# Pooling sums by accumulating DMAs, block-diagonal q and low weight parts on VectorE in an attention and feed-forward kernel on one core

## The chip, the core and the metric

One core of a Trainium2 chip runs the whole program. A core has TensorE (PE; its weight loads are listed as PEld), VectorE (DVE), ScalarE (ACT), GpSimd (POOL) and SyncE (SP), which here only issues DMAs. Each has a queue of its own and works through it in order; semaphores let one wait for another. 16 DMA engines move data between the memory outside (HBM) and the on-chip memory SBUF. TensorE writes its results to a second on-chip memory, PSUM.

The metric is the device time of one execution in microseconds, as the median of several runs. The profile shows one execution; its span runs from the first to the last instruction of the program, and the time of a run contains a few microseconds more around it.

## The reference

Eight batches, eight heads, 576 positions, 64 values per head. Two attentions are added: one over positions pooled by four (q, k and v averaged over four neighbours, 144 positions, full softmax), repeated four times along the positions, and a local one in which a position sees its neighbours at a distance below four. The sum goes through a feed-forward layer of 512 -> 2048 -> 512 with a leaky step.

```python
q_d = q.reshape(B, H, Sd, factor, D).mean(axis=3)      # factor = 4, Sd = 144
k_d = k.reshape(B, H, Sd, factor, D).mean(axis=3)
v_d = v.reshape(B, H, Sd, factor, D).mean(axis=3)
out_d = sm_attn(q_d, k_d, v_d)
out_up = np.repeat(out_d, factor, axis=2)
mask = np.abs(pos[:, None] - pos[None, :]) < factor
scores = np.where(mask, scale * np.matmul(q, k.transpose(0, 1, 3, 2)), -1e9)
out_local = np.matmul(softmax(scores), v)
x = (out_up + out_local).transpose(0, 2, 1, 3).reshape(B * S, H * D)   # 4608 x 512
h = x @ w_in
return np.maximum(0.01 * h, h) @ w_out
```

## The kernel before

**Stages.** The columns of x (4608 of them, one per position) are cut into chunks. Chunks 0 and 1 (256 and 320 columns) are batch 1; chunks 2 to 12 (256, 320, then 384 each) are cut from batches 2 to 8. In the code batches count from 0, so batch 2 is `b == 1`, and `BANDED = 1` says that batch 1 alone takes the banded way (local attention by matmuls, `banded`). For the others the local attention is done on POOL and DVE: `scores` multiplies q with seven shifted k on POOL (L560) and sums on DVE (L566), a softmax of small steps follows, `values` multiplies and sums again (L621, L627), and `landing` turns the result on PE (L658), adds the pooled part (L665) and splits it into a high part xh on ACT (L671) and a low part xl on DVE (L673). One unit of this work is a segment of at most `MAXSEG` blocks (a block is 64 columns) and one half `u` of the heads, with one load each of q, k and v. Tiles q, k and v have one buffer each, so a load of k waits for the last product that reads the one before.

**Feed-forward.** x and the weights are split into high and low parts of a fast matmul type, and each product is made of three matmuls: `up_proj` (L698), the leaky step on ACT (L708, L709) and DVE (L711), `down_proj` (L738). Chunks 0 and 1 pass over the first and the second half of the 2048 hidden values apart, as the weights arrive; each later chunk takes one pass. x has two buffers, so chunk n+2 is filled while chunk n+1 is used.

**Weights.** `convert` loads a quarter of w_in (k = 0) or of w_out (k = 1) at a time into a staging tile (it borrows the buffers of k, v, prod, up and, early, of chunk 1's x), rebuilds the values on ACT (L266) and DVE (L268), writes the high part on ACT (w_in, L279) or DVE (w_out, L276) and the low part `lo` on POOL (L281), 32 times in all. The last of these ends at 113 us, and the first product L560 follows it.

**Pooled attention.** `pooled(b, c)` handles two heads (c of NC = 4). `fetch` loads q and k side by side, [128, 2, 576], and v as [72, 2, 2, 64, 4] with the four neighbours innermost. For batches 2 to 8 DVE sums the four neighbours (L338 into qk_d, L380 into v_d). PE makes scores in six products of 64 rows and 64 columns each, one per head and third of q (L351). The softmax works over PSUM on DVE and ACT, three transposes of weights per half go through PE (L390) and ACT (L392), and four products mix v_d (L402); ACT copies the result out (L407) to outd. `widen` repeats it four times (L645).

**What sets the order.** The program is written out by a planner (`Order`) that runs at build time: each piece of work is a generator that yields its engine and an estimated duration; the planner takes the piece that can start first (then by its rank given to `spawn`) and so fixes the order of every engine's queue. Estimates: `COST` per engine, `pe(...)` in microseconds, `load` with 300 kB per microsecond. On the chip the queues are in order, so where something takes longer than planned, all behind it on that engine waits. SP's queue holds all loads and stores.

```python
t = yield from op("DVE", 1152, tq, s_qd.t)
nc.vector.tensor_reduce(out=qk_d, in_=qkr, axis=AX.X, op=ALU.add)              # L338
nc.tensor.matmul(sc[rows, qi * SD:(qi + 1) * SD], qk_d[rows, qi * QB:qi * QB + 64],
                 qk_d[rows, SD:2 * SD], start=True, stop=True)                  # L351, six times
nc.vector.tensor_reduce(out=v_d, in_=vs, axis=AX.X, op=ALU.add)                # L380
```

Of the kernel before, what the change touches and what calls it, by code (L numbers as in the profile page):

```python
# [19 lines left out]
FAC = 4  # L20
# [6 lines left out]
SCALE = 1.0 / D ** 0.5  # L27
MAXSEG = 4
SIZES = (4, 5, 6, 6, 6, 6, 6, 6, 6, 6, 6)
QB = 48  # L30
# [45 lines left out]
HOP = 0.2  # L76
SAFE = 0.4
SCARCE, HURRY = ("pt",), 1000

# [100 lines left out]
@with_exitstack  # L180
def attn_moe(ctx: ExitStack, tc, qkt, vd, qb, kb, vb, vwb, band, identb, w_in, w_out, ident, edge, out):
    nc = tc.nc
# [4 lines left out]

    bufs = dict(head=HEADS, qk=1, vs=1, qk_d=2, v_d=1, su_vd=2, su_half=1, st_d=2, pd=2, ptd=1, outd=2, q=1, k=1, v=1, s=3, st_l=3, prod=2, up=1,
                xloc=2, lst=3, gh=3, gl=3, o=2, hp=2, pt=2, xh0=1, xl0=1, xh1=1, xl1=1, acc0=1, acc1=1, acc2=1, acc3=1,
# [24 lines left out]
    def load(out, in_, size, *after):  # L214
        t = yield ("op", "SP", 0.3, max((0.0,) + after), size)
        nc.sync.dma_start(out=out, in_=in_)
        return t

# [31 lines left out]
    for h in heads:  # L250
        nc.vector.memset(h, 0)

    def convert(f, k):
# [27 lines left out]
        nc.gpsimd.tensor_tensor(out=lo, in0=tf, in1=hi.bitcast(F32), op=ALU.subtract)  # L281
        s.free(t)
# [24 lines left out]

    def fetch(b, c, pool):
        if pool is None:
            sq, sv = (yield from slot(*(("qk", "up") if b < BANDED else ("qk",)))), (yield from slot("vs"))  # L310
            qk, vs = sb(sq, [128, 2, S], F32), sb(sv, [72, 2, 2, D, FAC], F32)
        else:
            sq, sv = None, (yield from slot("su_vs"))
            qk = pool.tile([128, 2, S], F32, name=f"qk{c}")
            vs = sb(sv, [72, 2, 2, D, FAC], F32, pool)
        tq = yield from load(qk, qkt[b, c], 590e3, sq.t if sq else 0.0)
        od.signal(("asked", b, c))
        kept[b, c] = qk
        od.signal(("qk", b, c), tq)
        tv = yield from load(vs, vd[b, c], 295e3, sv.t if sv else 0.0)  # L320
        return sq, sv, qk, vs, tq, tv

    def pooled(b, c, rank, pool=None):
        sq, sv, qk, vs, tq, tv = yield from fetch(b, c, pool)
        s_qd = yield from slot("qk_d")
        qk_d = sb(s_qd, [128, 2 * SD], F32)
        qkr = qk.rearrange("p a (s r) -> p (a s) r", r=FAC)
        if b < BANDED and (b, c) != (0, 0):
            s = yield from slot("su_half")
            half = sb(s, [128, 2 * SD, 2], F32, pool)  # L330
            t = yield from op("POOL", 576, tq, s.t, s_qd.t)
            nc.gpsimd.tensor_tensor(out=half, in0=qkr[:, :, :2], in1=qkr[:, :, 2:], op=ALU.add)
            t = yield from op("POOL", 288, t)
            nc.gpsimd.tensor_tensor(out=qk_d, in0=half[:, :, 0], in1=half[:, :, 1], op=ALU.add)
            s.free(t)
        else:
            t = yield from op("DVE", 1152, tq, s_qd.t)
            nc.vector.tensor_reduce(out=qk_d, in_=qkr, axis=AX.X, op=ALU.add)  # L338
        if sq:
            if b < BANDED:  # L340
                od.spawn(rank, keeper(b, c, sq, t))
            else:
                sq.free(t)
# [3 lines left out]
        t = yield from pe(0.9, t, s_b.t)  # L347
        for qi in range(3):
            for p in range(2):
                rows = slice(64 * p, 64 * p + 64)  # L350
                nc.tensor.matmul(sc[rows, qi * SD:(qi + 1) * SD], qk_d[rows, qi * QB:qi * QB + 64],  # L351
                                 qk_d[rows, SD:2 * SD], start=True, stop=True)
        s_qd.free(t)
        scv = sc[:, :3 * SD].rearrange("p (a s) -> p a s", a=3)
        st, pd = sb(s_st, [128, 2, 3], F32), sb(s_pd, [128, 3, SD], F32)
# [20 lines left out]
        s_st.free(t)  # L376
        s_vd = yield from slot("su_vd" if pool else "v_d")
        v_d = sb(s_vd, [72, 2, 2, D], F32, pool)
        td = yield from op("DVE", 1050, tv, s_vd.t)
        nc.vector.tensor_reduce(out=v_d, in_=vs, axis=AX.X, op=ALU.add)  # L380
        if sv:
            sv.free(td)
# [12 lines left out]
        s_pd.free(tt)  # L395
        to = yield from wait(("outd", b))
        s_b = yield from slot("pt")
        av = bank(s_b)
        t = yield from pe(0.68, te, td, s_b.t)
        for p in range(2):  # L400
            for kc in range(2):
                nc.tensor.matmul(av[64 * p:64 * p + 64, :SD], v_d[:, p, kc], ptd[:, kc, p],  # L402
                                 start=kc == 0, stop=kc == 1)
        s_pt.free(t)
        s_vd.free(t)
        t = yield from op("ACT", 144, t, to)
        nc.scalar.copy(out=outd[b][:, c], in_=av[:, :SD])  # L407
        s_b.free(t)
        od.signal(("pooled", b, c), t)
        if b == 0:  # L410
# [4 lines left out]
    def windows(c, hf, pool):  # L415
        b0, b1 = BLKS[hf]
        s_vw = yield from slot("su_vs" if hf else "su_vw")
        vws[c, hf] = s_vw, sb(s_vw, [WIN, 5, 2, D], F32, pool)
        t = yield from load(vws[c, hf][1][:, :b1 - b0], vwb[0, c, :, b0:b1], 35840 * (b1 - b0), s_vw.t)
        od.signal(("vw", c, hf), t)  # L420
# [370 lines left out]
    with tc.manual_schedule():  # L791
        od.spawn(0, fixed())
        for b in range(B):
            od.spawn(0, outd_tile(b))
# [86 lines left out]
```

## Time and profile before

| | |
|---|---|
| time of three runs | 970.41, 975.27, 976.92 us, median 975.27 |
| span of the profiled execution (its own whole time is not on the page) | 965.5 us |
| PE, DVE, ACT, POOL busy | 936.8, 594.7, 415.6, 611.5 us |
| first projection matmul | 48.5 us |
| last low part of a weight, first product L560 | 113.2, 113.3 us |
| first up projection of chunks 2, 3, 4, 5, 12 | 185.7, 242.0, 306.1, 378.7, 885.1 us |
| last landing of chunk 12 (L673) | 832.8 us |
| last POOL instruction ends | before 808 us |

The page has the span in 40 slices of 24 us; each digit is the busy share of an engine in tenths, PEclk the clock granted to TensorE, DMA the busy share of the DMA engines.

```profile
PE   6699999899999999999999999999999999999997
DVE  5897778767876786687667883872753752411111
ACT  3777655434634454345524552532422423422211
POOL 3655766777989788897889785884685783200000
PEclk9689999999999999999999999999999999999999
DMA  9857656434542543446233542351233221000000
```

How to read it: the first two slices are the start, in which batch 1's attention is done and the first weights arrive; from there on PE is nearly always busy. POOL is at 7 to 9 tenths from slice 7 to the middle and done in slice 34. A row of an engine's list or timeline has the source line, the engine, the operation, the output tile and the inputs, and the shapes (partitions x elements); a busy matmul is shown longer than the distance to the next one, since matmuls overlap, so the distance between starts is what one costs.

### The profile page before, as it was taken

How to read it: one execution, taken by the hardware profiler on the slowest of the kernel's cores; microseconds unless marked ns; L12 is line 12 of the kernel's file. 1: busy time of each engine (PE TensorE's matmuls, PEld its weight loads, DVE VectorE, ACT ScalarE, POOL GpSimd, SP SyncE). 2: the span in 40 equal slices, each digit the busy share in tenths (PEclk: the TensorE clock that was granted, in tenths of full speed). 3: DMA queues.
4: the chain of work that ended last, by engine and by line, in shares of the span. 5: the costliest groups of instructions: out<-in, count | busy, mean ns of one | idle time of the engine just before them, and what ended most of it. 6: DMA issues, size and time to landing. Idle time of an engine off the chain costs nothing.

```text
span 965.5 us, 16163 instructions
## 1 busy us (share of the span) xinstructions
PE 936.8 (97%) x6282; PEld 897.8 (93%) x6282; DVE 594.7 (62%) x895; ACT 415.6 (43%) x1139; POOL 611.5 (63%) x356
## 2 busy tenths in 40 slices
PE   6699999899999999999999999999999999999997
PEld 4499999799999999999999899999999999999997
DVE  5897778767876786687667883872753752411111
ACT  3777655434634454345524552532422423422211
POOL 3655766777989788897889785884685783200000
PEclk9689999999999999999999999999999999999999
DMA  9857656434542543446233542351233221000000
GB/s 261 249 189 238 211 175 196 145 121 136 191 128 87 187 141 105 128 152 188 91 115 115 189 150 96 98 154 60 75 90 99 91 62 46 34 1 1 33 1 33
DMA packets 63180, 117.31 MB, mean 122 GB/s; under 512 B 4944, under 2 KB 32848, under 8 KB 63104
## 3 DMA queue, kind: packets, MB, share of 16 engines
q1 hardware_dynamic: 63104, 116.29, 38.6%
q8 instruction: 49, 0.80, 0.3%
q14 instruction: 27, 0.22, 0.1%
HBM read 105.65 MB, written 10.62 MB: 120 GB/s over the span
## 4 chain that ended last, share of the span: by engine, by line
PE 79%; DMA 8%; POOL 7%; DVE 3%; issue 2%; SPq 1%; ACT 0%; POOLq 0%; DVEq 0%; ACTq 0%
PE hp L698 36%; PE acc L738 35%; POOL prod L560 4%; DMA k<-in_kb_dram 3%; POOL prod L621 2%; PE pt L351 2%; DMA qk<-in_qkt_dram 2%; PE pt L390 2%; PE pt L402 1%; DMA v<-in_w_out_dram 1%; PE pt L658 1%; DMA out_dram<-o 1%; DMA su_vw<-in_vwb_dram 1%; DVE s L566 1%; DMA v<-in_vb_dram 1%
## 5 line engine op out<-in xcount | busy, mean ns | idle before, releaser
L560 POOL TENSOR_TENSOR prod<-q,k 128x1344 f32<-128x1344 f32 (+1 forms) x88 | 260.2, 2958 | 93.3 <-DMA k<-in_kb_dram 61.4
L698 PE MATMUL hp<-xh,wih 128*128 128x384 f32 (+2 forms) x832 | 278.7, 335 | 5.1 <-DVE gl L711 5.0
L621 POOL TENSOR_TENSOR prod<-v,s 128x1344 f32<-128x1344 f32 (+1 forms) x88 | 265.3, 3017 | 25.4 <-DVE xloc L627 16.0
L738 PE MATMUL acc<-gh,woh 128*128 128x384 f32 (+2 forms) x832 | 274.8, 330 | 0.6 <-DVE o L763 0.2
L698 PE MATMUL hp<-xl,wih 128*128 128x384 f32 (+2 forms) x832 | 269.5, 324 | 0.0
L698 PE MATMUL hp<-xh,wil 128*128 128x384 f32 (+2 forms) x832 | 269.4, 324 | 0.0
L738 PE MATMUL acc<-gh,wol 128*128 128x384 f32 (+2 forms) x832 | 269.4, 324 | 0.0
L738 PE MATMUL acc<-gl,woh 128*128 128x384 f32 (+2 forms) x832 | 269.4, 324 | 0.0
L708 ACT ACTIVATE gh<-hp 128x384 fp32r<-128x384 f32 (+2 forms) x208 | 97.3, 468 | 318.2 <-PE acc L738 303.6
L711 DVE TENSOR_TENSOR gl<-hp,gh 128x384 fp32r<-128x384 f32 (+2 forms) x208 | 108.3, 522 | 200.4 <-ACT hp L709 198.3
L698 PEld LDWEIGHTS hp<-xh,wih 128*128 128x128 f32 x832 | 157.1, 189 | 13.6 <-DVE gl L711 7.0
L738 PEld LDWEIGHTS acc<-gh,woh 128*128 128x128 f32 x832 | 156.3, 188 | 3.8 <-issue 2.2
L698 PEld LDWEIGHTS hp<-xl,wih 128*128 128x128 f32 x832 | 157.3, 189 | 0.0
L698 PEld LDWEIGHTS hp<-xh,wil 128*128 128x128 f32 x832 | 157.0, 189 | 0.0
L738 PEld LDWEIGHTS acc<-gl,woh 128*128 128x128 f32 x832 | 156.5, 188 | 0.0
L738 PEld LDWEIGHTS acc<-gh,wol 128*128 128x128 f32 x832 | 156.2, 188 | 0.0
L566 DVE TENSOR_REDUCE s<-prod 128x21 f32<-128x1344 f32 (+1 forms) x88 | 130.5, 1483 | 33.1 <-POOL prod L560 33.0
L627 DVE TENSOR_REDUCE xloc<-prod 128x192 f32<-128x1344 f32 (+1 forms) x88 | 130.3, 1481 | 30.1 <-POOL prod L621 29.8
L709 ACT ACTIVATE hp<-hp 128x384 f32<-128x384 f32 (+2 forms) x208 | 96.4, 463 | 0.0
L665 DVE TENSOR_TENSOR pt<-pt,up 128x384 f32<-128x384 f32 (+1 forms) x44 | 38.1, 865 | 31.7 <-PE pt L658 29.0
L645 ACT COPY up<-outd 128x576 f32<-128x576 f32 x84 | 52.3, 675 | 0.0
L338 DVE TENSOR_REDUCE qk_d<-qk 128x288 f32<-128x1152 f32 x29 | 39.0, 1346 | 13.6 <-DMA qk<-in_qkt_dram 13.6
(111 smaller groups left out, 748.9 us busy)
## 6 DMA issues: line engine op xcount, KB each, us to landing
k<-in_kb_dram SPq DMA_DIRECT2D x38, 576.0 KB
v<-in_vb_dram SPq DMA_DIRECT2D x38, 576.0 KB
qk<-in_qkt_dram SPq DMA_DIRECT2D x32, 576.0 KB
vs<-in_vd_dram SPq DMA_DIRECT2D x28, 288.0 KB
q<-in_qb_dram SPq DMA_DIRECT2D x38, 192.0 KB
out_dram<-o SPq DMA_DIRECT2D x36, 192.0 KB
prod<-in_w_out_dram SPq DMA_DIRECT2D x8, 512.0 KB
k<-in_w_in_dram SPq DMA_DIRECT2D x4, 512.0 KB
```

The costliest lines, as they stand in the source:

```text
L338: nc.vector.tensor_reduce(out=qk_d, in_=qkr, axis=AX.X, op=ALU.add)
L560: nc.gpsimd.tensor_tensor(out=prv, in0=q[:, p, a - j0:z - j0].unsqueeze(2).to_broadcast([128, n, W, D]), in1=view(k[:, p], (a - j0) * D, [ ...
L566: nc.vector.tensor_reduce(out=s[:, p, a - j0:z - j0], in_=prv, axis=AX.X, op=ALU.add)
L621: nc.gpsimd.tensor_tensor(out=prv, in0=view(v[:, p], a - j0, [[1, n], [nv, D], [1, W]]), in1=s[:, p, a - j0:z - j0].unsqueeze(2).to_broadc ...
L627: nc.vector.tensor_reduce(out=xl_t[:, :n, p], in_=prv, axis=AX.X, op=ALU.add)
L645: nc.scalar.copy(out=up[:, pp], in_=outd[b][:, 2 * u + pp].unsqueeze(2).to_broadcast([128, SD, FAC]))
L665: nc.vector.tensor_tensor(out=xv, in0=xv, in1=upv, op=ALU.add)
L698: nc.tensor.matmul(hp[:, :n], wt[:, c], x[:, c], start=k == 0, stop=k == 3 * NC - 1)
L708: nc.scalar.activation(out=gh[:, :n], in_=hp[:, :n], func=AF.Prelu, alpha=0.01)
L709: nc.scalar.activation(out=hp[:, :n], in_=hp[:, :n], func=AF.Prelu, alpha=0.01)
L711: nc.vector.tensor_tensor(out=gl[:, :n], in0=hp[:, :n], in1=gh[:, :n].bitcast(F32), op=ALU.subtract)
L738: nc.tensor.matmul(acc[:, :n], wt[:, es], g[:, :n], start=f == f0 and j == 0, stop=f == f1 - 1 and j == 2)
```

## The change

Seven edits, all for batches 2 to 8 except the last:

1. **Sums by DMA.** The host lays q and k out as [batch, neighbour, 128, c, 288] (`qka`) and v alike (`va`). Per batch, `sums` loads the first neighbour of all four c with SP into `qd` and `vdd`, and then issues three DMAs for each of the two tiles from POOL that add the next neighbour into SBUF (`accumulate`). Each waits for the one before on its tile. In all 42 such DMAs; the bytes read from HBM for pooling stay the same. L338 and L380 fall away for these batches, and with them their buffers. There is one qd and one vdd, so a batch's first load waits until the scores (or the mixing) of the batch before are done.
2. **Block-diagonal q.** `cleared` sets two tiles [128, 3, 128] to zero on POOL once; for each c ACT copies q of the two heads into the two diagonal blocks (two copies of 64x144), and three products with all 128 rows and columns replace the six.
3. **Mixing in pairs.** Two c share one PSUM bank: eight products, then one copy of 288 columns on ACT.
4. **Segments.** MAXSEG is 3 instead of 4. All segments but one had at most three blocks; the first, of 4 blocks, becomes 2 + 2.
5. **Buffers.** ptd has two instead of one, q, k and v shrink with MAXSEG, and batch 1's qk_d moves to the memory of the start.
6. **Planner.** Scores are estimated at 1.07 us (batch 1) and 0.75, mixing at 0.3 + 0.45 per c, an accumulating DMA at 1.0 us of POOL.
7. **Low parts of w_out** (k = 1 in `convert`, 16 of 32) are subtracted on DVE instead of POOL, for all weights.

```diff
-MAXSEG = 4
+MAXSEG = 3
+ISSUE = 1.0
...
+    def accumulate(out, in_, size, *after):
+        t = yield ("op", "POOL", ISSUE, max((0.0,) + after) + SAFE, size)
+        nc.gpsimd.dma_start(out=out, in_=in_, accum_op=ALU.add)
+        return t
...
-        t = yield from op("POOL", 590, t)
-        nc.gpsimd.tensor_tensor(out=lo, in0=tf, in1=hi.bitcast(F32), op=ALU.subtract)
+        if k:
+            t = yield from op("DVE", 512, t)
+            nc.vector.tensor_tensor(out=lo, in0=tf, in1=hi.bitcast(F32), op=ALU.subtract)
+        else:
+            t = yield from op("POOL", 590, t)
+            nc.gpsimd.tensor_tensor(out=lo, in0=tf, in1=hi.bitcast(F32), op=ALU.subtract)
...
+    def sums(b):
+        yield from (wait(("x", 0), NC) if b == BANDED else wait(("summed", b - 1)))
+        sq, sv = (yield from slot("qd")), (yield from slot("vdd"))
+        qd, vdd = sb(sq, [128, NC, 2 * SD], F32), sb(sv, [72, NC, 2, 2, D], F32)
+        tq = yield from load(qd, qka[b - BANDED, 0], 590e3, sq.t)
+        tv = yield from load(vdd, va[b - BANDED, 0], 295e3, sv.t)
+        for r in range(1, FAC):
+            tq = yield from accumulate(qd, qka[b - BANDED, r], 590e3, tq)
+            tv = yield from accumulate(vdd, va[b - BANDED, r], 295e3, tv)
+        summed[b] = qd, vdd
+        od.signal(("summed", b), max(tq, tv))
+        sq.free((yield from wait(("scored", b), NC)))
+        sv.free((yield from wait(("mixed", b), NC // 2)))
...
+            q_d, k_d = qblks[s_qd.index % len(qblks)], qd[:, c, SD:]
+            for p in range(2):
+                rows = slice(64 * p, 64 * p + 64)
+                t = yield from op("ACT", 144, t)
+                nc.scalar.copy(out=q_d[rows, :, 64 * p:64 * p + QB], in_=qd[rows, c, :SD].rearrange("p (a s) -> p a s", a=3))
...
+            if b >= BANDED:
+                nc.tensor.matmul(sc[:, qi * SD:(qi + 1) * SD], q_d[:, qi], k_d, start=True, stop=True)
+                continue
...
+        for i, (_, _, _, pt_i, v_i, _) in enumerate(mine):
+            for p in range(2):
+                for kc in range(2):
+                    nc.tensor.matmul(av[64 * p:64 * p + 64, i * SD:(i + 1) * SD], v_i[:, p, kc], pt_i[:, kc, p],
+                                     start=kc == 0, stop=kc == 1)
...
+            od.spawn(85 + 10 * b, sums(b))
```

How the queues change, at three places. The first is POOL's queue in the start, before (low parts L281 of both weights, wil of w_in and wol of w_out, between the last steps of batch 1's band, L480):

```order
L480 TENSOR_TENSOR xloc<-xloc,lst 128x350
L281 TENSOR_TENSOR wol_69<-k,woh_68 128x512
L281 TENSOR_TENSOR wil_67<-xl_103,wih_66 128x512
L281 TENSOR_TENSOR wil_67<-v,wih_66 128x512
L281 TENSOR_TENSOR wol_69<-prod,woh_68 128x512
L480 TENSOR_TENSOR xloc<-xloc,lst 128x350
L281 TENSOR_TENSOR wil_67<-prod,wih_66 128x512
L281 TENSOR_TENSOR wol_69<-up,woh_68 128x512
```

And POOL's queue at the same place in the changed kernel (L222 is the accumulating DMA, L298 the low part, L540 the band's step):

```order
L222 DMA qd<-in_qka_dram 128x1152
L222 DMA vdd<-in_va_dram 72x1024
L540 TENSOR_TENSOR xloc<-xloc,lst 128x350
L298 TENSOR_TENSOR wil_67<-prod,wih_66 128x512
L222 DMA qd<-in_qka_dram 128x1152
L222 DMA vdd<-in_va_dram 72x1024
L298 TENSOR_TENSOR wil_67<-prod,wih_66 128x512
L222 DMA qd<-in_qka_dram 128x1152
L298 TENSOR_TENSOR wil_67<-k,wih_66 128x512
L222 DMA vdd<-in_va_dram 72x1024
```

The low parts of w_out are gone from POOL, and batch 2's six accumulating DMAs stand between those of w_in.

The second is ACT's queue in the start, before (L266 rebuilds weights, L279 writes their high part, L392 and L407 belong to batch 2's first c, L490 to the band, L708 is the leaky step):

```order
L392 COPY ptd<-pt 72x3x2x48
L266 CAST head_71<-k 128x512
L279 CAST wih_66<-up 128x512
L407 COPY outd<-pt 128x144
L490 COPY su_pt<-pt 70x384
L708 ACTIVATE gh<-hp 128x256
```

And in the changed kernel (L365 copies q into the block-diagonal tiles, L768 is the leaky step):

```order
L292 CAST wih_66<-up 128x512
L365 COPY qblk_74<-qd 64x3x48
L365 COPY qblk_75<-qd 64x3x48
L279 CAST head_71<-k 128x512
L550 COPY su_pt<-pt 70x256
L550 COPY su_pt<-pt 70x384
L768 ACTIVATE gh<-hp 128x256
```

The copies of q, which wait for the last of batch 2's sums of q, now stand ahead of weight work and of a leaky step on ACT.

The third is SP's queue while chunk 3 is made, before (qk and vs are one c's loads for pooling; q, k and v the loads of the local attention):

```order
L216 DMA qk<-in_qkt_dram 128x1152
L216 DMA vs<-in_vd_dram 72x1024
L216 DMA q<-in_qb_dram 128x2x128
L216 DMA k<-in_kb_dram 128x2x512
L216 DMA qk<-in_qkt_dram 128x1152
L216 DMA vs<-in_vd_dram 72x1024
L216 DMA v<-in_vb_dram 128x2x576
```

And in the changed kernel:

```order
L217 DMA q<-in_qb_dram 128x2x192
L217 DMA k<-in_kb_dram 128x2x576
L217 DMA v<-in_vb_dram 128x1152
L217 DMA q<-in_qb_dram 128x2x128
L217 DMA k<-in_kb_dram 128x2x512
L217 DMA v<-in_vb_dram 128x1152
L217 DMA out_dram<-o 128x320 x2
L217 DMA o<-out_dram 128x320 x2
L217 DMA q<-in_qb_dram 128x2x128
L217 DMA k<-in_kb_dram 128x2x512
L217 DMA qd<-in_qka_dram 128x1152
```

Loads for pooling stand on SP once a batch (qd and vdd) instead of once a c, and loads of values no longer stand behind a vs that waits for its buffer.

More of the change, by code (lines that the diff above doesn't have):

```diff
@@ L180, in attn_moe @@
 @with_exitstack
-def attn_moe(ctx: ExitStack, tc, qkt, vd, qb, kb, vb, vwb, band, identb, w_in, w_out, ident, edge, out):
+def attn_moe(ctx: ExitStack, tc, qkt, vd, qka, va, qb, kb, vb, vwb, band, identb, w_in, w_out, ident, edge, out):
     nc = tc.nc
@@ L186, in attn_moe @@
     ps = ctx.enter_context(tc.tile_pool(name="ps", bufs=1, space=PSUM))
-    bufs = dict(head=HEADS, qk=1, vs=1, qk_d=2, v_d=1, su_vd=2, su_half=1, st_d=2, pd=2, ptd=1, outd=2, q=1, k=1, v=1, s=3, st_l=3, prod=2, up=1,
+    bufs = dict(head=HEADS, qd=1, vdd=1, qk_d=2, qblk=2, su_vd=2, su_half=1, st_d=2, pd=2, ptd=2, outd=2, q=1, k=1, v=1, s=3, st_l=3, prod=2, up=1,
                 xloc=2, lst=3, gh=3, gl=3, o=2, hp=2, pt=2, xh0=1, xl0=1, xh1=1, xl1=1, acc0=1, acc1=1, acc2=1, acc3=1,
@@ L251, in attn_moe, with cleared @@
         nc.vector.memset(h, 0)
+    qblks = [const.tile([128, 3, 128], F32, name=f"qblk{i}") for i in range(bufs["qblk"])]
+    def cleared():
+        yield from wait(("x", 0), NC)
+        for t in qblks:
+            nc.gpsimd.memset(t, 0)
+            od.signal("cleared", (yield from op("POOL", 200, 0.0)))
     def convert(f, k):
@@ L306, in x_tile @@
         s_l.free(t)
[L308 to L311, printed above, removed]
-        else:
[L313 to L341, printed above, removed]
-            else:
-                sq.free(t)
+    def fetch(c, pool):
+        sv = yield from slot("su_vs")
+        qk = pool.tile([128, 2, S], F32, name=f"qk{c}")
+        vs = sb(sv, [72, 2, 2, D, FAC], F32, pool)
+        tq = yield from load(qk, qkt[0, c], 590e3)
+        od.signal(("asked", 0, c))
+        kept[0, c] = qk
+        od.signal(("qk", 0, c), tq)
+        tv = yield from load(vs, vd[0, c], 295e3, sv.t)
+        return sv, qk, vs, tq, tv
@@ new lines, in attn_moe, with pooled @@
+    halves = {}
+    def pooled(b, c, rank, pool=None):
+        if b >= BANDED:
+            tq = yield from wait(("summed", b))
+            qd, vdd = summed[b]
+            yield from wait("cleared", len(qblks))
+            s_qd = yield from slot("qblk")
+            q_d, k_d = qblks[s_qd.index % len(qblks)], qd[:, c, SD:]
+            t = max(tq, s_qd.t, od.events["cleared"][1])
+            for p in range(2):
+                rows = slice(64 * p, 64 * p + 64)
+                t = yield from op("ACT", 144, t)
+                nc.scalar.copy(out=q_d[rows, :, 64 * p:64 * p + QB], in_=qd[rows, c, :SD].rearrange("p (a s) -> p a s", a=3))
+        else:
+            sv, qk, vs, tq, tv = yield from fetch(c, pool)
+            qkr = qk.rearrange("p a (s r) -> p (a s) r", r=FAC)
+            s_qd = yield from slot("qk_d")
+            qk_d = sb(s_qd, [128, 2 * SD], F32, pool)
+            if c:
+                s = yield from slot("su_half")
+                half = sb(s, [128, 2 * SD, 2], F32, pool)
+                t = yield from op("POOL", 576, tq, s.t, s_qd.t)
+                nc.gpsimd.tensor_tensor(out=half, in0=qkr[:, :, :2], in1=qkr[:, :, 2:], op=ALU.add)
+                t = yield from op("POOL", 288, t)
+                nc.gpsimd.tensor_tensor(out=qk_d, in0=half[:, :, 0], in1=half[:, :, 1], op=ALU.add)
+                s.free(t)
+            else:
+                t = yield from op("DVE", 1152, tq, s_qd.t)
+                nc.vector.tensor_reduce(out=qk_d, in_=qkr, axis=AX.X, op=ALU.add)
@@ L353, in pooled @@
         s_qd.free(t)
+        if b >= BANDED:
+            od.signal(("scored", b), t)
         scv = sc[:, :3 * SD].rearrange("p (a s) -> p a s", a=3)
@@ L376, in pooled @@
         s_st.free(t)
[L377 to L381, printed above, removed]
+        if b >= BANDED:
+            v_d, td, s_vd = vdd[:, c], tq, None
+        else:
+            s_vd = yield from slot("su_vd")
+            v_d = sb(s_vd, [72, 2, 2, D], F32, pool)
+            td = yield from op("DVE", 1050, tv, s_vd.t)
+            nc.vector.tensor_reduce(out=v_d, in_=vs, axis=AX.X, op=ALU.add)
             sv.free(td)
@@ L396, in pooled @@
         to = yield from wait(("outd", b))
+        mine = [(c, s_pt, s_vd, ptd, v_d, max(te, td))]
+        if b >= BANDED:
+            if c % 2 == 0:
+                halves[b, c] = mine[0]
+                od.signal(("half", b, c))
+                return
+            yield from wait(("half", b, c - 1))
+            mine.insert(0, halves.pop((b, c - 1)))
+        c0, n = mine[0][0], len(mine)
         s_b = yield from slot("pt")
         av = bank(s_b)
[L399 to L407, printed above, removed]
+        t = yield from pe(0.3 + 0.45 * n, s_b.t, *(x[5] for x in mine))
+        for i, (_, _, _, pt_i, v_i, _) in enumerate(mine):
[3 more added lines that the diff above has]
+                                     start=kc == 0, stop=kc == 1)
+        for x in mine:
+            x[1].free(t)
+            if x[2]:
+                x[2].free(t)
+        if b >= BANDED:
+            od.signal(("mixed", b), t)
+        t = yield from op("ACT", 144 * n, t, to)
+        nc.scalar.copy(out=outd[b][:, c0:c0 + n], in_=av[:, :n * SD].rearrange("p (c s) -> p c s", c=n))
         s_b.free(t)
-        od.signal(("pooled", b, c), t)
+        for x in mine:
+            od.signal(("pooled", b, x[0]), t)
         if b == 0:
```

14 lines of the change are left out of this document (10 added, 4 removed).

## The prediction

> **What bounds the kernel now.** I read the page's busy times first, then the busy times by stage, then the timeline at the places where a chunk's x lands.
>
> ```profile
> span 965.5 us, 16163 instructions
> PE 936.8 (97%) x6282; PEld 897.8 (93%) x6282; DVE 594.7 (62%) x895; ACT 415.6 (43%) x1139; POOL 611.5 (63%) x356
> ```
> PE is busy 97% of the span, so TensorE's own work is the first bound. By stage (columns: stretch, length, then busy time and instructions of PE, weight load, DVE, ACT, POOL, then the granted clock, DMA share, GB/s):
>
> ```profile
> 48.50:113.30 64.80, 64.44 (x562) 60.76 (x561) 52.49 (x85) 46.87 (x114) 37.85 (x29) 0.95 0.71 222
> 242.00:306.00 64.00, 63.47 (x462) 61.48 (x461) 48.01 (x70) 30.53 (x91) 56.21 (x30) 1.00 0.44 138
> ```
> Up to 306 us the busy PE hides a second bound. The first up projection of chunks 3 and 4 starts within a microsecond of the last landing of their x (L673 on DVE); chunk 5, at 378.69, starts 10 us after it (368.70):
>
> ```profile
> 242.20 0.42 DVE L673 TENSOR_TENSOR xl<-pt,xh 128x256 fp32r<-128x256 f32 x1 [0.45 <-ACT xh L671]
> 242.03 0.31 PE L698 MATMUL hp<-xh,wih 128*128 128x320 f32 x1
> 304.68 0.56 DVE L673 TENSOR_TENSOR xl<-pt,xh 128x384 fp32r<-128x384 f32 x1 [0.55 <-ACT xh L671]
> 306.11 0.34 PE L698 MATMUL hp<-xh,wih 128*128 128x384 f32 x1
> 368.14 0.56 DVE L673 TENSOR_TENSOR xl<-pt,xh 128x384 fp32r<-128x384 f32 x1
> 378.69 0.34 PE L698 MATMUL hp<-xh,wih 128*128 128x384 f32 x1
> ```
> So until 306 the path that makes x (loads, POOL products, DVE sums, landings) sets the pace, and only after it a microsecond less of PE is a microsecond off the end. POOL, 88% busy there (56.21 of 64.00), sets that path.
>
> **PE: scores and mixing.** An isolated group of scores, an isolated group of mixing (v_d with the turned weights), and three transposes of the full array:
>
> ```profile
> 327.93 0.34 PE L738 MATMUL acc<-gh,wol 128*128 128x384 f32 x1
> 328.20 0.95 PE L351 MATMUL pt<-qk_d 64*64 64x144 f32 x12
> 329.08 0.44 PE L698 MATMUL hp<-xh,wih 128*128 128x384 f32 x1
> 329.36 0.34 PE L698 MATMUL hp<-xl,wih 128*128 128x384 f32 x1
> ...
> 320.85 0.34 PE L738 MATMUL acc<-gh,wol 128*128 128x384 f32 x1
> 321.11 0.72 PE L402 MATMUL pt<-ptd,v_d 72*64 72x144 f32 x8
> 321.76 0.44 PE L698 MATMUL hp<-xh,wih 128*128 128x384 f32 x1
> 322.04 0.34 PE L698 MATMUL hp<-xl,wih 128*128 128x384 f32 x1
> ...
> 348.02 0.33 PE L738 MATMUL acc<-gh,wol 128*128 128x384 f32 x1
> 348.20 0.49 PE L390 MATMUL pt<-id_sb,pd 128*72 128x128 f32 x3
> 348.44 0.42 PE L738 MATMUL acc<-gh,woh 128*128 128x384 f32 x1
> 348.70 0.34 PE L738 MATMUL acc<-gl,woh 128*128 128x384 f32 x1
> ...
> L351 PE MATMUL pt<-qk_d x168: 282/283/334, 328.2 to 635.4; 64*64 64x144 f32 x168
> L402 PE MATMUL pt<-ptd,v_d x128: 286/286/338, 321.1 to 644.3; 72*64 72x144 f32 x128
> ```
> Two projection matmuls stand 0.175 us apart, so the scores cost 329.36-327.93-0.35 = 1.08 us, for six products in twelve records of 0.061 us ((0.95-0.28)/11); some 0.35 of it is the change of tile at both ends. Mixing costs 322.04-320.85-0.35 = 0.84 us. The transposes, which use the whole array, cost 348.70-348.02-0.35 = 0.33 us, 0.11 each, and no change of tile. Block-diagonal q makes three products of 128 columns in place of six of 64. No such product is in the trace. If its two records overlap as the 64-wide ones do, three cost 3 x 0.124 = 0.37 (0.124 is 0.11 for 144 columns instead of 128); if they follow each other, 0.74. I take 0.74: a record of 64 columns leaves room beside it, one of 128 does not, like the transposes. Saving 0.34 a group (0.71 at the low end). Mixing two c in one group drops one change of tile, 0.84 - 4 x 0.124 = 0.35 a pair.
>
> After 306 us stand 14 groups of scores (168 records, 12 each) and 8 pairs of mixing (128 records, 16 a pair): 14 x 0.34 + 8 x 0.35 = **-7.6 us**. The other 14 groups and 6 pairs of batches from the second on, 6.9 us, lie ahead of 306 and count only if x lands earlier.
>
> **The x path, from the first product (113.3) to chunk 4.** Removed: DVE's sums and what waits for them.
>
> ```profile
> L338 DVE TENSOR_REDUCE qk_d<-qk 128x288 f32<-128x1152 f32 x29 | 39.0, 1346 | 13.6 <-DMA qk<-in_qkt_dram 13.6
> L380 DVE TENSOR_REDUCE v_d<-vs 72x256 f32<-72x1024 f32 x28 | 33.6, 1198 | 0.6 <-PE pt L402 0.6
> ...
> 165.29 7.08 DMA qk<-in_qkt_dram
> ...
> 180.32 1.22 DVE v_d L380
> ...
> 181.97 5.35 DMA v<-in_vb_dram
> ...
> 192.56 0.39 PE L698 MATMUL hp<-xh,wih 128*128 128x256 f32 x1 [2.79 <-DVE gl L711]
> ```
> These rows of the chain are one story: a late qk holds DVE, DVE's late v_d holds SP's load of vs, the values load queued behind it on SP comes late, POOL and DVE wait, and PE stands 2.79 us. That chain goes. Added, by POOL's new order: fourteen accumulating DMAs up to chunk 4's last product (42 in all, six ahead of this stage), two more segments (4 blocks become 2+2, so 38 loads of k become 40), each with one more wait for its k, and 56 copies of q on ACT. POOL's waits in the stage, and the nearest prices of an issue and of a copy:
>
> ```profile
>   DMA k<-in_kb_dram: 18.8, 11
> POOL s L573 <- DVE s L566: 7.5, 4, 3.0
> POOL s L580 <- DVE st_l L578: 6.8, 6, 1.6
> POOL prod L621 <- DMA v<-in_vb_dram: 4.1, 2, 3.7
> 1.19 0.42 SPq L216 DMA_DIRECT2D idb_sb<-in_identb_dram  x1
> L281 POOL TENSOR_TENSOR wol<-prod,woh x8: 1297/1438/1832, 38.5 to 108.1; 128x512 fp32r<-128x512 f32 x8
> L407 ACT COPY outd<-pt 128x144 f32<-128x144 f32 x32 | 9.0, 280 | 25.7 <-PE pt L402 25.7
> ```
> No POOL issue is in the trace; SP's takes 0.42, POOL's low part 1.4; I take 1.0, between them: 14 us. POOL waits 1.7 us for k eleven times (18.8 us), and an issue that falls there is free: half, -7. Two segments more: 2 x (1.7 + 0.8 for three small steps) = +5. Of the 18.4 us that POOL waits for DVE and for values here (7.5 + 6.8 + 4.1) I take half as gone, since DVE loses 2.5 us (1.346 + 1.198) for every c: -9. Sum **+3 us**, between -13 (all issues hidden, all those waits gone) and +19 (neither). SP's qd load waits for the last scores of the batch before, once a batch where vs waited four times. ACT is 48% busy (30.53 of 64.00), so copies of some 0.28 us cost nothing there while their sums are in time; the two clears of the q tiles and the second ptd buffer lie in POOL's and ACT's idle time.
>
> **The start, 48 to 113 us.** Sixteen low parts leave POOL (16 x 1.4 = 23 us); DVE gets sixteen operations with two SBUF inputs, 0.68 to 1.80 us each by its own operation of that kind, and gives up batch 2's sums. Batch 2's sums come instead as a chain on POOL, between band products and low parts of the first weight (the POOL rows shown with the change). Each qd waits for the landing of the one before, and the low parts of the first weight wait behind it on POOL. On ACT, the copies of q wait for the last sum, with weight heads and the leaky step (gh, hp) queued behind.
>
> ```profile
> 0.74 3.90 DMA qk<-in_qkt_dram
> L268 DVE SCALAR_TENSOR_TENSOR prod<-prod,head x12: 681/933/1804, 31.4 to 104.4; 128x512 int32<-128x512 int32 x12
> ```
> A transfer of these 590 kB took 3.90 us on an empty wire and 7.08 in the stage above; an accumulating one also reads its target, so 3.9 to 14.2 us. I take 7.1: POOL is blocked 3 x 7.1 less 8 us of work between, 13 us. In amount it is covered: POOL idles 64.80-37.85 = 27 us here and loses low parts. What it delays (first weights, gh) is not all covered: **+3 us**, between -5 (products start sooner, since POOL is lighter) and +14. The Trainium skill, "DMA: Bandwidth & Descriptors", section "Anatomy of one DMA", gives 2.0 us plus bytes/436e3 for a POOL-issued DMA, an estimate of 3.4 us here; by that the block nearly vanishes and the time would be 971. The trace agrees for an empty wire (3.90), not under load (7.08).
>
> **Sum.** 965.5 - 7.6 + 3 + 3 = 963.9 us of span. The three runs shown have a median of 975.27, 9.8 above this span (the page has no whole time of the profiled execution); with it, **973.7 us**.
>
> **Rivals.**
> *Faster:* x lands as early as PE allows, issues hide in the waits for k. Then the 6.9 us ahead of 306 count too: 965.5-14.5+9.8 = 960.8, less if wide products overlap. For it: the chain at 165 to 192 goes. Against: POOL has little slack before 306.
> *Slower, by in-order waits on POOL and ACT:* accumulates that land after 10 us or more. POOL's block in the start is no longer covered and products start up to 14 us late, and after it the issues find no wait to hide in (14+5-9 = +10): 965.5-7.6+14+10+9.8 = 991.7. It decides from about 10 us a landing; POOL having slack of 10 us at chunk 5 speaks against more.
> *Slower, by DVE holding POOL's issues:* a low part on POOL has 1.3 us alone and 1.8 at most, L268 0.68 and 1.80, so the two engines do stretch each other. If each of the 20 issues before chunk 4 waits for a DVE sum (1.2 us), half of it beside other waits, +12: 985.7. The Trainium skill, "SBUF — State Buffer", "Who interferes with whom", says that descriptor writing on POOL is blocked while VectorE holds the shared port pair, but that reductions never take it; no run here shows a POOL issue.
> *No cheaper scores:* each wide record paced by its weight load; then 14 x 0.34 = 4.8 us stay: 978.5.
>
> **Chances.** Forecast 0.39, no cheaper scores 0.04 (both within 1%), faster 0.26, in-order waits 0.24, DVE holding 0.07. One per cent is about what a measurement of this kernel can tell from none. Faster by over 1% 0.26, within 0.43, slower 0.31. Range 957 (the faster case with cheaper wide products) to 994 (both slower cases); outside some 0.2.
>
> **What would show it.** Wide score groups of 0.74 us with no longer step behind them; mixing pairs at 1.33; POOL's waits for k shorter and first product near 113; chunk 4's up projection at its last landing near 306, the rest about 7 us shorter. Wrong if PE stands over 5 us between 55 and 110 behind gh, if POOL waits long on its own DMAs, or if chunk 5 also starts at its landing.

## The result, and the profile after

The changed kernel takes **986.53 us** (median of 4 runs, 984.64 to 989.86), the kernel before 972.84 us (4 runs, 968.02 to 976.92): a ratio of 1.0136, interval 1.0104 to 1.0169. It is slower by 1.4%, where 973.7 was forecast and "within 1%" had the largest chance.

The run whose profile is shown took 985.56 us for a span of 983.6, so about 2 us lie around a span. The profiled execution of the kernel before (965.5) must then have taken some 967.5: it was one of its fastest. The two profiles are 18.1 us apart, the medians only 13.7; so some 4 us of what the profiles show between them lie within the spread of the runs.

The head of the page of the changed kernel, busy time and instructions of each engine:

```profile
span 983.6 us, 15802 instructions
PE 933.9 (95%) x6114; PEld 908.1 (92%) x6114; DVE 540.5 (55%) x861; ACT 429.3 (44%) x1189; POOL 624.5 (63%) x390
```

TensorE's busy time is not longer than before (933.9 us where it had 936.8) and yet it ends 18 us later: it stands more. Split at POOL's first product (L560, now L620) and at chunk 4's start, the spans differ by -3.8 us up to the product (113.3 and 109.5), +13.6 from there to chunk 4 (192.8 and 206.4) and +8.3 behind it. The first place to look at is chunk 4, whose x lands and whose up projection starts here (timeline: start, length, engine, line, operation, and idle time with what ended it):

```profile
314.71 0.56 DVE L733 TENSOR_TENSOR xl<-pt,xh 128x384 fp32r<-128x384 f32 x1
315.88 0.34 PE L758 MATMUL hp<-xh,wih 128*128 128x384 f32 x1
```

It was 304.68 and 306.11 before: 9.8 us later. The second place is behind it. From chunk 4's start to the end of the span the kernel before needs 965.5 - 306.1 = 659.4 us, the changed one 983.6 - 315.9 = 667.7, and two gaps of TensorE stand in this stretch, at 330.68 and at 413.75:

```profile
330.68 0.34 PE L758 MATMUL hp<-xh,wil 128*128 128x384 f32 x1
335.46 0.69 PE L798 MATMUL acc<-gh,woh 128*128 128x384 f32 x1 [4.44 <-ACT o L832]
...
413.75 0.34 PE L758 MATMUL hp<-xh,wil 128*128 128x384 f32 x1
416.90 0.69 PE L798 MATMUL acc<-gh,woh 128*128 128x384 f32 x1 [2.81 <-ACT o L832]
```

Both times the down projection of a new chunk waits for an accumulator bank, because ScalarE's copy of the old sums into o (L832) is late. Each gap costs more than its length: behind it the clock granted to TensorE is 0.50 for some 3 us, and products start 0.32 us apart where 0.175 is usual. That adds 1.4 us behind the first gap (nine steps, 335.46 to 338.45) and 1.6 behind the second. The timeline, and the row of a stretch with its granted clock (third number from the end):

```profile
336.27 0.52 PE L798 MATMUL acc<-gh,wol 128*128 128x384 f32 x1
336.59 0.52 PE L798 MATMUL acc<-gh,woh 128*128 128x384 f32 x1
...
336.00:337.00 1.00, 1.00 (x5) 1.00 (x4) 1.00 (x1) 0.00 (x0) 1.00 (x2) 0.50 0.67 247
```

TensorE's busy time contains such stretches: in the first run below, without these gaps, the same 6114 instructions are busy for 924.2 us instead of 933.9.

The chain of waits (start, length, what) says why, and also shows what made x late:

```profile
142.24 8.84 DMA qd<-in_qka_dram
...
155.86 6.78 DMA o<-out_dram
...
227.09 8.10 DMA v<-in_vb_dram
...
260.04 5.13 DMA v<-in_vb_dram
...
274.78 5.63 DMA v<-in_vb_dram
...
289.96 8.94 DMA v<-in_vb_dram
...
326.21 8.69 DMA out_dram<-o
334.98 0.43 ACT o L832
...
407.84 8.45 DMA out_dram<-o
```

There are two o buffers. The third copy of a pass waits until the store of the first has landed, and that store, 160 or 192 KB, now takes 8.4 to 8.7 us; two stores in the chain of the kernel before took 2.75 and 5.15. The loads of v at 227.09 and 289.96 take 8.1 and 8.9 us, each with additions issued within 0.8 us of it; the two between them, with none near, take 5.1 and 5.6, and the chain of the kernel before had 5.35 for one. What the late ones share the wire with are the new transfers (page, DMA issues: KB of each and median us to landing; last line the queue with packets, MB and its share of 16 engines' span):

```profile
qd<-in_qka_dram POOLq DMA_DIRECT2D x21, 576.0 KB, 8.3
vdd<-in_va_dram POOLq DMA_DIRECT2D x21, 288.0 KB, 6.5
q0 software_dynamic: 5040, 18.58, 10.7%
```

One of 576 KB is issued at 290.10, 0.14 us behind the load of v at 289.96 (and one at 325.12, a microsecond ahead of the stores):

```profile
289.96 0.34 SPq L217 DMA_DIRECT2D v<-in_vb_dram  x1
...
290.10 0.87 POOL L222 DMA_DIRECT2D qd<-in_qka_dram  x1
290.74 1.14 POOL L222 DMA_DIRECT2D vdd<-in_va_dram  x1
293.61 3.10 POOL L620 TENSOR_TENSOR prod<-q,k 128x1344 f32<-128x1344 f32 x1 [1.73 <-DMA k<-in_kb_dram]
299.04 3.15 POOL L681 TENSOR_TENSOR prod<-v,s 128x1344 f32<-128x1344 f32 x1 [2.33 <-DMA v<-in_vb_dram]
```

The waits of the two kernels for o, before the change and then after it, there with two waits for qd (engine, line, what it waited for: us in total, times, longest):

```profile
ACT o L772 <- DMA out_dram<-o: 12.5, 10, 2.5
PE acc L738 <- ACT o L772: 0.2, 1, 0.2
```

```profile
ACT o L832 <- DMA out_dram<-o: 21.1, 10, 3.9
PE acc L798 <- ACT o L832: 7.8, 3, 4.4
PE acc L798 <- DVE o L823: 7.5, 1, 7.5
POOL qd L222 <- DMA qd<-in_qka_dram: 15.1, 6, 4.1
ACT qblk L365 <- DMA qd<-in_qka_dram: 7.3, 2, 7.1
```

The wait of 7.5 us is TensorE's longest gap. It lies ahead of chunk 4, from 155.3 on: VectorE waits with an addition to old sums (L823) for the load of o that stands in the chain at 155.86.

What TensorE was to save is there. An isolated group of scores and one of mixing:

```profile
367.12 0.34 PE L798 MATMUL acc<-gh,wol 128*128 128x384 f32 x1
367.30 0.90 PE L388 MATMUL pt<-qd,qblk 128*128 128x144 f32 x6
367.94 0.44 PE L758 MATMUL hp<-xh,wih 128*128 128x384 f32 x1
368.21 0.33 PE L758 MATMUL hp<-xl,wih 128*128 128x384 f32 x1
...
370.28 0.33 PE L758 MATMUL hp<-xh,wil 128*128 128x384 f32 x1
370.54 1.25 PE L457 MATMUL pt<-ptd,vdd 72*64 72x144 f32 x16
371.72 0.44 PE L798 MATMUL acc<-gh,woh 128*128 128x384 f32 x1
372.00 0.34 PE L798 MATMUL acc<-gl,woh 128*128 128x384 f32 x1
```

By the reckoning of the prediction the scores cost 368.21 - 367.12 - 0.35 = 0.74 us (1.08 before) and a pair of mixings 372.00 - 370.28 - 0.35 = 1.37 (2 x 0.84 before).

### The profile page after: what moved, and what is told of

Same layout as the page of the kernel before. It is cut to its first block, busy times and chain, and to the rows that moved or that the text cites. A ratio compares the mean times of both kernels' runs of the same rounds, so it can differ in the third digit from the quotient of the medians.

```text
span 983.6 us, 15802 instructions
## 1 busy us (share of the span) xinstructions
PE 933.9 (95%) x6114; PEld 908.1 (92%) x6114; DVE 540.5 (55%) x861; ACT 429.3 (44%) x1189; POOL 624.5 (63%) x390
## 3 DMA queue, kind: packets, MB, share of 16 engines
q0 software_dynamic: 5040, 18.58, 10.7%
## 4 chain that ended last, share of the span: by engine, by line
PE 51%; DMA 19%; POOL 18%; issue 5%; DVE 3%; ACT 2%; SPq 1%; POOLq 0%; DVEq 0%; ACTq 0%
PE acc L798 24%; PE hp L758 23%; POOL prod L620 10%; POOL prod L681 6%; DMA k<-in_kb_dram 6%; DMA qd<-in_qka_dram 5%; DMA v<-in_vb_dram 3%; DMA out_dram<-o 2%; SPq L217 1%; PE pt L388 1%; DMA k<-in_w_in_dram 1%; DMA k<-in_w_out_dram 1%; DMA su_vs<-in_vd_dram 1%; PE pt L718 1%; PE pt L435 1%
## 5 line engine op out<-in xcount | busy, mean ns | idle before, releaser
L620 POOL TENSOR_TENSOR prod<-q,k 128x1344 f32<-128x1344 f32 (+1 forms) x88 | 264.0, 3000 | 77.8 <-DMA k<-in_kb_dram 50.1
L798 PE MATMUL acc<-gh,woh 128*128 128x384 f32 (+2 forms) x832 | 277.6, 334 | 15.3 <-ACT o L832 7.8
L768 ACT ACTIVATE gh<-hp 128x384 fp32r<-128x384 f32 (+2 forms) x208 | 97.4, 468 | 336.8 <-PE acc L798 331.9
L798 PEld LDWEIGHTS acc<-gh,woh 128*128 128x128 f32 x832 | 158.7, 191 | 17.5 <-ACT o L832 8.7
L798 PEld LDWEIGHTS acc<-gl,woh 128*128 128x128 f32 x832 | 158.8, 191 | 0.1
L798 PEld LDWEIGHTS acc<-gh,wol 128*128 128x128 f32 x832 | 158.3, 190 | 0.0
L705 ACT COPY up<-outd 128x576 f32<-128x576 f32 x88 | 54.8, 675 | 0.0
L437 ACT COPY ptd<-pt 72x288 f32<-72x288 f32 x64 | 25.3, 398 | 29.3 <-PE pt L435 29.3
```

What stands on the lines that cost most here:

```text
L437: nc.scalar.copy(out=ptd[:, kc].rearrange("k p a q -> k a p q"), in_=tp[0:72, :384].rearrange("k (a p q) -> k a p q", a=3, p=2)[:, :, :, :QB])
L620: nc.gpsimd.tensor_tensor(out=prv, in0=q[:, p, a - j0:z - j0].unsqueeze(2).to_broadcast([128, n, W, D]), in1=view(k[:, p], (a - j0) * D, [ ...
L705: nc.scalar.copy(out=up[:, pp], in_=outd[b][:, 2 * u + pp].unsqueeze(2).to_broadcast([128, SD, FAC]))
L768: nc.scalar.activation(out=gh[:, :n], in_=hp[:, :n], func=AF.Prelu, alpha=0.01)
L798: nc.tensor.matmul(acc[:, :n], wt[:, es], g[:, :n], start=f == f0 and j == 0, stop=f == f1 - 1 and j == 2)
```

## The experiments

Three theories stood after this. *Issue theory*: POOL's time for 42 issues makes x late. *Wire theory*: the accumulating transfers fill the DMA engines, and loads and output stores land late. *Order theory*: shorter segments, other positions and weight parts on VectorE are the loss. Medians in us; the ratio is to runs of the kernel before on the same chip. Those have medians between 972.4 and 974.6, so a difference between two rows can be off by a microsecond or two; the ratios are the better measure for small ones.

| run | median | ratio to before, 95% interval |
|---|---|---|
| changed kernel | 986.5 | 1.0136 (1.0104 to 1.0169) |
| no accumulating DMA | 958.3 | 0.9847 (0.9807 to 0.9886) |
| thin accumulating DMA | 959.6 | 0.9855 (0.9820 to 0.9889) |
| plain writes from POOL | 972.4 | 0.9986 (0.9963 to 1.0010) |
| plain writes from SyncE | 964.8 | 0.9922 (0.9894 to 0.9951) |
| changed, four o | 975.4 | 1.0040 (1.0004 to 1.0077) |
| plain from POOL, four o | 966.6 | 0.9937 (0.9913 to 0.9962) |
| changed, low parts on POOL | 993.3 | 1.0214 (1.0163 to 1.0265) |
| before + low parts on VectorE | 976.1 | 1.0039 (1.0012 to 1.0066) |
| before + segments of three | 972.2 | 0.9987 (0.9973 to 1.0002) |
| ... + wide scores | 967.1 | 0.9940 (0.9915 to 0.9966) |
| ... + wide scores + low parts | 960.8 | 0.9870 (0.9845 to 0.9895) |
| ... + wide scores + low parts + pairs | 960.4 | 0.9862 (0.9841 to 0.9884) |

**The transfers taken out, thinned, made plain.** In the first three runs only the line that emits the DMA differs; the planner still counts it, so every other instruction keeps its place.

```diff
 def accumulate(out, in_, size, *after):
     t = yield ("op", "POOL", ISSUE, max((0.0,) + after) + SAFE, size)
-    nc.gpsimd.dma_start(out=out, in_=in_, accum_op=ALU.add)
     return t
```

> The 42 accumulating DMAs are left out (batches from the second on get a quarter of each sum), the order of all other instructions and their estimates stay. Changed kernel: span 983.6 us, chunk 4's first up projection at 315.9, PE standing in gaps over 0.45 us for some 9.6 us after it, against 306.1 and 0.8 us before the change. Issue theory (POOL's time for the issues is what makes x late): chunk 4 near 305, the stalls after it stay, span about 973. Wire theory (accumulates fill the DMA engines, output stores land late behind them and TensorE stands for its accumulator banks): stalls after chunk 4 fall below 2 us, chunk 4 moves by less than 4 us, span about 975. Both: about 963. Order theory (shorter segments, later groups and weight parts on VectorE are the loss): 980 to 984.

```diff
-    nc.gpsimd.dma_start(out=out, in_=in_, accum_op=ALU.add)
+    w = (slice(None), 0, 0, 0, slice(0, 16)) if len(out.shape) == 5 else (slice(None), 0, slice(0, 16))
+    nc.gpsimd.dma_start(out=out[w], in_=in_[w], accum_op=ALU.add)
```

> Each accumulating DMA adds only 16 columns (64 bytes a partition) of its tile, so that POOL issues as many from the same places and waits for their landings, but the wire carries almost nothing; the sums are left incomplete. Issue theory: as the changed kernel up to chunk 4 (up projection near 316), span 975 to 984. Wire theory: stalls after chunk 4 under 2 us, and if late loads of k and v behind accumulates also make x late, chunk 4 near 306 and the span near 965. Order theory: 980 to 984.

```diff
-    nc.gpsimd.dma_start(out=out, in_=in_, accum_op=ALU.add)
+    nc.gpsimd.dma_start(out=out, in_=in_)
```

> The same 42 transfers, full size, from the same places on POOL, but plain writes instead of additions (the tile ends with the last quarter alone, the sums are left out). If it is the bytes and POOL's issues, it is as the changed kernel: 982 to 985, landings of 8 us and stores of 8 us. If it is the addition, which takes the DMA engines longer per byte, landings fall to some 4 to 6 us, the output stores to 4 us, and the span to 973 to 977. Order theory: 980 to 984.

Without the transfers it takes 958.3, 28 us less, more than any theory expected. With all 42 issues and their waits but almost no bytes it takes 959.6: 1.3 us more, with intervals that overlap. The issue theory falls. With the bytes, written plainly, 972.4 (+12.8); with the bytes added, 986.5 (+14.1). All three came out lower than any theory had named. Chunk 4's up projection starts at 295.4, 299.2, 305.2 and 315.9 in the profiles of the four. By these profiles the bytes cost 5.9 us in front of chunk 4's start and 8.2 behind it, the addition 10.7 in front and 3.0 behind. The kernel before reads the bytes for pooling too, from SyncE's queue, so the 12.8 are not all new with the change. The DMA issues and the queue of the thin run, then of the plain one:

```profile
qd<-in_qka_dram POOLq DMA_DIRECT2D x21, 8.0 KB, 4.0
q0 software_dynamic: 5040, 0.27, 0.9%
```

```profile
qd<-in_qka_dram POOLq DMA_DIRECT2D x21, 576.0 KB, 5.9
q0 software_dynamic: 5040, 18.58, 5.8%
```

The engines' time, as shares of all 16: the same 18.58 MB take 5.8% of 969.9 us = 56 us when written and 10.7% of 983.6 = 105 us when added: 1.87 times as long. At the place shown above (v issued next to an addition, then POOL's product), the thin run, with the same order, has no wait for v:

```profile
276.57 0.34 SPq L217 DMA_DIRECT2D v<-in_vb_dram  x1
...
276.65 0.88 POOL L223 DMA_DIRECT2D qd<-in_qka_dram  x1
...
280.88 3.10 POOL L621 TENSOR_TENSOR prod<-q,k 128x1344 f32<-128x1344 f32 x1 [2.09 <-DMA k<-in_kb_dram]
283.94 3.14 POOL L682 TENSOR_TENSOR prod<-v,s 128x1344 f32<-128x1344 f32 x1
```

**Four buffers for the stores.**

```diff
-    bufs = dict(..., qblk=2, ..., pd=2, ..., o=2, ...)
+    bufs = dict(..., qblk=1, ..., pd=1, ..., o=4, ...)
```

> The changed kernel with four buffers for output stores in place of two (room for them from one q tile and one softmax tile less). The copies of the accumulators then need not wait for the stores of the same pass to land. Wire theory, store part: TensorE's stalls after chunk 4 (9.6 us in the changed kernel) fall to under 3 us and the time to 977 to 980. If the stores were only the place where the lateness shows and x is next in line, it stays within 3 us of the changed kernel's 986.5. One tile less of q and of softmax could cost up to 3 us.

975.4: 11.1 us come back (9.4 by the ratios; the ten runs lie between 972.4 and 983.2), a little more than expected. The profile has no wait of TensorE for o any more; all that is left of waits at o is

```profile
ACT o L832 <- PE acc L798: 10.8, 5, 4.8
DVE o L829 <- PE acc L798: 4.3, 2, 3.8
DVE o L823 <- PE acc L798: 1.3, 2, 1.0
```

while the additions take as long as in the changed kernel (8.7 and 7.1 us). Four buffers thus give back most of the 13.7 us by which the change is slower than the kernel before, but less than half of the 26.9 that bytes and additions cost together (975.4 against 959.6 of the thin run). In the profiles one half of the gain lies behind chunk 4 (661.3 us to the end, 667.7 without), the other in front of it (chunk 4 at 309.5, not 315.9). The order also moved with the buffers, and the kernel before was not run with four, so not every microsecond can be put to late stores.

**Where plain bytes come from, and both cures together.** The first has `nc.sync.dma_start(out=out, in_=in_)` in place of the addition, the second the plain write from POOL with four o.

> As the run with plain writes in place of the additions (972.4), but the 42 transfers are issued by SyncE, in the same places of the order, and so stand in one queue with the loads of k and v and the output stores; the sums are left out. The version with sums on VectorE moves as many bytes, all from SyncE, and took 960.8: if it is the second queue that makes plain bytes dear, 958 to 964. If the bytes are dear wherever they come from, 970 to 974. SyncE now waits for each quarter to land before it issues the next, with loads of k and v behind it: if that decides, 975 or more.

> Plain writes from POOL in place of the additions, with four buffers for output stores: the sums are left out. Four buffers took the changed kernel from 986.5 to 975.4, plain writes took it to 972.4. If both are the same loss (stores that land late), the two together stay at 968 to 973. If the stores are the loss of the bytes and the late loads of v that of the addition, they add up: 960 to 964.

From SyncE's queue the same bytes cost 964.8 - 959.6 = 5.2 us and not 12.8, although SyncE waits for each quarter (6.5 us by the ratios). That lies just above the 958 to 964 of the second queue, and below the 970 to 974 of bytes that are dear wherever they come from: from POOL's queue they cost some 6 to 8 us more. The run changes the queue and the issuing engine at once, so which of the two it is stays open. The two cures together give 966.6, between "the same loss" and "they add up": four buffers save 5.8 with plain writes and 11.1 with additions (4.8 and 9.4 by the ratios).

**Low parts back on POOL**, `if k:` and its VectorE branch taken out of the conversion of weights:

> The low parts of the second weight go back to POOL (16 x 1.4 = 23 us of it before the first product), all else stays. If VectorE's part of the change is a loss (order theory), chunk 2's x lands no later than 181 and the span falls by 2 to 6 us, to 978 to 982. If it is what made chunk 2's x land 5 us earlier than before the change, chunk 4 moves from 315.9 to 321 or more and the span to 987 to 994. No effect within 2 us if the first products wait for loads.

993.3, 6.8 us slower. This part of the change earns something there; the order theory falls for it. But it does not earn it as expected: chunk 4 starts at 316.2, where 321 or more had been named, as early as in the changed kernel. The 7.3 us more lie behind it (675.0 to the end of the span), where TensorE's waits for o are 11.1 us instead of 7.8. How much of the worth is the low parts' own and how much the place of the stores in another order is not shown.

**Parts of the change on the kernel before.** Low parts on VectorE alone; segments alone (`MAXSEG = 3`); then segments, wide scores and low parts, with the sums still on VectorE:

> The kernel before with one part of the change alone: low parts of the second weight on VectorE. Putting them back on POOL cost the changed kernel 6.8 us. If that worth carries over, 966 to 969 where the kernel before has 974. If VectorE's sums for batch 2, which the kernel before still has in the start, are in the way, 972 to 980.

> The kernel before with segments of at most three blocks alone (one step of four blocks becomes two of two, 40 loads of k to chunk 4 where there were 38). By my term of +5 us for the x path it is 978 to 980 where the kernel before has 974; order theory 980 or more; if POOL's waits hide it, 973 to 976.

```diff
+        if b >= BANDED:
+            yield from wait("cleared", len(qblks))
+            s_qb = yield from slot("qblk")
+            q_d = qblks[s_qb.index % len(qblks)]
+            t = max(t, s_qb.t, od.events["cleared"][1])
+            for p in range(2):
+                rows = slice(64 * p, 64 * p + 64)
+                t = yield from op("ACT", 144, t)
+                nc.scalar.copy(out=q_d[rows, :, 64 * p:64 * p + QB], in_=qk_d[rows, :SD].rearrange("p (a s) -> p a s", a=3))
...
+            if b >= BANDED:
+                nc.tensor.matmul(sc[:, qi * SD:(qi + 1) * SD], q_d[:, qi], qk_d[:, SD:2 * SD], start=True, stop=True)
+                continue
```

> The kernel before (sums on VectorE, plain loads, mixing one c at a time) with segments of at most three blocks, block-diagonal q for scores and low parts on VectorE: the change without its accumulating DMAs and pairs. Wire theory: the DMA bytes are those of the kernel before and none of them is added in SBUF, so 974 - 7 (low parts) - 5 (14 score groups after chunk 4 at 0.35 us less) = 962, and not over 968. Order theory (segments and wide scores cost something in their own right): 974 or more.

Segments cost nothing (972.2, interval across 1). Low parts alone cost a little (976.1), where 966 to 969 had been expected from the run above. The three together give **960.8, faster than both kernels**: the change without its accumulating DMAs and pairs. The span of its profile is 959.6 us, TensorE busy for 928.4 and VectorE for 602.0.

Two more runs take this apart: the same with the low parts on POOL, and the same with pairs of mixing (room from one softmax tile and one tile of sums).

> As the version with sums on VectorE, wide scores and segments of three (960.8), but with the low parts of the second weight on POOL as in the kernel before: it leaves segments and wide scores as the only parts of the change. If the low parts on VectorE are worth what they were to the changed kernel, 966 to 968; if they are worth nothing or cost a little, as when done alone (976.1 against 973.3), 958 to 962, and the gain of 12.5 us is the wide scores' (segments alone gave 972.2).

> As the version with sums on VectorE, wide scores, segments of three and low parts on VectorE (960.8), and the mixing of two c in one group as well (room from one softmax tile and one tile of sums less). Pairs save 1.70 - 1.38 = 0.32 us each, 8 after chunk 4: 2.6 us, so 957 to 959 if TensorE is the bound there; 960 to 964 if the single buffers hold back the scores.

Wide scores alone are worth 972.2 - 967.1 = 5.1 us, low parts beside them 967.1 - 960.8 = 6.3, pairs 0.4, which these runs cannot tell from nothing; the run with pairs also has the single buffers that the expectation named as what could hide them. Why low parts on VectorE gain 6.3 and 6.8 us beside wide scores but lose about 2.8 in the kernel before stays open.

## Why the prediction was wrong

- **What bounds the kernel** was right: x until chunk 4, TensorE after it. Chunk 4 starts with its last landing (x complete at 315.3), chunk 5 not (383.4 against 397.9).
- **Scores and mixing, -7.6**: the prices were right, 0.74 a group and 1.37 a pair (1.33 forecast), and in the runs on the kernel before wide scores gave 5.1 us, near 14 x 0.34 = 4.8. That the gain lies where the sum put it is not shown: with low parts on VectorE as well (960.8), chunk 4 starts at 301.3, 4.8 us earlier than before, and the stretch behind it, 658.3 us, is only 1.1 shorter. In the changed kernel the gain is hidden: 16 groups of scores stand behind chunk 4's start, where the kernel before has 14, and two gaps, 4.6 and 3.0 us beyond the usual step and 3.0 more at half the clock, stand against it. The pairs' 2.8 us did not show (0.4).
- **The x path, +3**: it came out at +13.6 (first product to chunk 4, 113.3 to 306.1 before and 109.5 to 315.9 after), all of it behind chunk 2 (whose x is complete at 186.4 before and 181.1 after). The step was "fourteen accumulating DMAs ... I take 1.0 ... 14 us. POOL waits 1.7 us for k eleven times, and an issue that falls there is free". An issue does take 0.99 us and mostly hides; all of them with their waits cost 1.3 us in the end. Two more segments, +5 in the sum, cost nothing. (There are two, but 42 loads of k become 44 in the whole kernel; 38 is the number of those for three blocks, not of those up to chunk 4.)
- **The start, +3**: it came out the other way. The first product is at 109.5 (113.3 before), chunk 2's x 5.3 us earlier. POOL waits 7.0 us for qd and 2.0 for vdd in this stage, where 13 was reckoned. Not all of it is free: in the thin run the first product is at 106.0. The low parts that left POOL give as much back (113.0 with them on POOL again).
- **The step that failed** is the price of a landing: "so 3.9 to 14.2 us. I take 7.1: POOL is blocked". The size was close (8.3 and 6.5). But it was put to one account, POOL's wait, and to the start alone; for the additions behind the first product the sum has their issue and no landing. The other account was left out: loads of v and output stores that run beside such a transfer take longer (8.1 to 8.9 us where others of their kind take 2.8 to 5.6), and the stores hold the two o buffers, ScalarE's copies, the accumulator banks and TensorE. The prediction costed every queue in which the transfers are issued and no queue that shares the wire with them. The runs price that account, with what waits for the longer landings, at 12.8 us for the bytes and 14.1 for adding them.
- **The rivals.** The slower one, in-order waits on POOL and ACT, named 991.7 and was near in time. It was to decide from landings of about 10 us; they take 8.3. Its start is refuted: the first product comes earlier, not up to 14 us later. Its waits are there: one of the prediction's signs of being wrong came, POOL waits 15.1 us for qd and 3.9 for vdd, against 3.8 for qd alone in the thin run, and ScalarE's copies of q wait 7.3. Six landings of qd lie in the chain, four of additions (from 46.50, 142.24, 601.89 and 611.25, 30.2 us in all) and two of a batch's first load (from 39.08 and 199.93, 14.8 us). With four o buffers POOL still waits 7.9 and 5.7, and 11.1 us are back. How much of the 15.8 us that remain over the thin run is POOL's and ScalarE's waiting and how much late loads was not tried apart, so this rival holds a part of unknown size. The VectorE rival shows nowhere: issues with all their waits cost 1.3 us. "No cheaper scores" is refuted by 0.74.
- **The estimate of a landing by the Trainium skill** ("DMA: Bandwidth & Descriptors", 3.4 us) is too low here, beside other traffic: 5.9 us written, 8.3 added. Another page bears on the addition: "Collectives: The Full Stack", section "The bandwidth ceiling: the fold count and why AG ≠ RS ≠ AR", says that an addition in the DMA path reads two sources for each write, so that a reducing phase has half the throughput of a copying one, 1.93 measured there. The 1.87 here is near it; the page speaks of collectives, not of loads, and no run here shows the two reads.
- **From span to time**: 9.8 us were added as what lies around the span. It is 2; the rest was that the profiled execution was a fast one. Set against the medians, the sum said -1.6 us and the measurement +13.7.

## What to carry to other kernels

A DMA that adds in SBUF is not free work: here it took the DMA engines 1.87 times as long as a plain one of the same bytes, and loads and stores beside it landed late. The two gaps of TensorE behind chunk 4 also cost more than their length, as its clock was halved for some 3 us behind each. Before moving sums onto the wire, look at which transfers stand beside them, above all output stores with few buffers, whose lateness reaches TensorE through the accumulators. Apply the parts of a change one by one: here wide scores and low parts on VectorE were worth 12.5 us, and the accumulating DMAs in the same change cost more than that (986.5 against 960.4 with the sums on VectorE).

## What the runs showed that was not expected

- The issue of a transfer that adds takes 0.99 us of POOL (means of 0.995 and 0.991 over 21 each), of a plain one of the same shape 0.57 to 0.59, and of the thin adding one 1.00 to 1.05. So in these runs the time goes with the addition and not with the bytes.
- Low parts of a weight on VectorE gain 6 to 7 us in one order of work and lose 3 in another.
- The same plain bytes cost 5.2 us from SyncE's queue and 12.8 from POOL's.
